# DeltaNet attention with a PReLU feed-forward on one core: weight sums moved from VectorE to GpSimd, late 32x32 products and output copies rearranged

## The chip, the core and the metric

The kernel runs on one core of a Trainium2 chip. A core has five engines, each with its own queue of instructions, worked off in order: TensorE (PE in the profile; its weight loads are shown apart as PEld), VectorE (DVE), ScalarE (ACT), GpSimd (POOL) and SyncE (SP), which here only issues DMAs. Engines wait for each other through semaphores. PE writes its products to PSUM, which has eight banks of 2 KB per partition; DVE and ACT read them from there, and GpSimd works on SBUF alone. The metric is the device time of one execution in microseconds (us).

## What is computed

Everything is float32. First a DeltaNet recurrence over 4 batches, 8 heads, 768 positions, head size 48; then, on the 3072 tokens of width 384 that this gives, a feed-forward of inner width 2048 with a PReLU:

```python
k_n = k / (norm(k) + 1e-6)
for t in range(768):
    y[t] = q[t] @ state                       # per batch and head, state is 48x48
    v_old = k_n[t] @ state
    state = state + beta[t] * outer(k_n[t], v[t] - v_old)
x = y transposed to (4 * 768, 8 * 48)
h = x @ w_in                                  # 384 -> 2048
g = max(h, 0) + alpha * min(h, 0)
out = g @ w_out                               # 2048 -> 384
```

## The kernel before

**Attention in steps.** The recurrence is worked in chunks of 64 positions (`C`). A step n is one chunk of two batches; 12 chunks times 2 pairs of batches give 24 steps, and two steps of one chunk belong to different pairs, so that each pair's state is handed on every other step. Within a chunk the recurrence becomes the inverse of a unit triangular 64x64 matrix for each of 16 batch-heads. Its 32x32 diagonal blocks are inverted on DVE for four steps at once, by column elimination (`eliminate`: 30 pairs of a multiplication, L593, and an addition, L599, both with two operands in SBUF, with transposes at L566 before and after). GpSimd prepares the block for it (L583, L587). The block off the diagonal needs two rounds of 32x32 products on PE (`products`, L733): one for step n+2, whose result ACT copies to `mid`, and one for step n+1, whose result ACT copies to `inv` (`copied`, L745).

**A step's products.** `burst_a(n)` issues to PE the outputs of step n-1 (`outputs`, L840), the product for the next state (`next_state`, L857), and `through_state` (L802). DVE then subtracts from the state (L865, tile `beside`), makes the right side `r` (three instructions at L812) and the masked product `a_t` (L521). `turn_round(n)` issues weights and transposes: DVE's reciprocal (L412) and two small GpSimd instructions (L418, L419) give the weights `wgt` of a later step. `burst_b(n)` issues the query (L784), `solve` (L827) and the 32x32 products; DVE turns the solution into `u` (L831), which the outputs of the next burst need. Up to step 14 `burst_b` also issues the gram product of step n+9 (L501, weighted by DVE at L507 into `same` and `right`). From step 8 on (`NARROW`) the outputs are copied from PSUM by ACT (L846), transposed by DVE (`turn_y`, L881) and put in place by ACT (`rows_y`, L894).

**The feed-forward fills the time between bursts.** The 12 chunks of 256 tokens pass through `ffn_in` (L996; ACT takes the negative part at L1006, DVE adds the two parts at L1008) and `ffn_out`. Chunks 0 and 1 use the plain second product (L1039). From chunk 2 on, `ffn_out_fast` (L1060) takes seven products where eight would be needed, with operands that are sums: of the activations (`operand_sums`, L950, DVE) and of `w_out` (`weight_sums`, L983, DVE, once: eight instructions of 128x768, four for each half b). From chunk 8 on `ffn_in_fast` does the same for the first product; its sums of `w_in` come from `input_sums` (L1162, DVE, once: eight of 128x512, made while chunk 7 passes `ffn_out_fast`). In `ffn_in_fast` ACT copies the shared products (L1264), GpSimd adds them up (L1269), and DVE adds them to the rest (L1274) and applies the slope (L1283).

**What sets the order.** The order on each engine is written out by hand: `weave` interleaves generators by a share of progress, and `stretch(n, ...)` runs n pieces of the feed-forward (`tail`) beside pieces of elimination, of `placing` (L704, L707, L718) and of the list `later` that a burst returns. An engine never overtakes its own queue. So GpSimd begins an instruction as soon as the one before it in its queue and the semaphores allow, whatever DVE is at by then.

**Where the changed pieces stand.** `weight_sums(0, 0, 3)` is woven into step 5, `weight_sums(1, 0, 3)` and `weight_sums(0, 3, 4)` into step 6, `weight_sums(1, 3, 4)` into step 7. Within a half the second sum needs the first, and the last one overwrites a quarter of `w_out`. The product that first reads all eight is in `ffn_out_fast(2)`. `input_sums` has the same form; its two last sums of each half overwrite parts of `w_in` and so must follow `ffn_in(7)`.

**PSUM.** From step 8 on there are two pairs of banks for attention and four single banks for the feed-forward. `ps_big()` hands the pairs out in turn. In `burst_b` the pair `b` takes the solution and the 32x32 products side by side, and the pair `x` takes the gram product and the query; the outputs are later added onto the query in the same columns, and `next_state` writes the first columns of the same pair. Instructions of two engines on one bank are kept apart by semaphores.

Of the kernel before, what the change touches and what calls it, by code (L numbers as in the profile page):

```python
# [28 lines left out]
ALU = mybir.AluOpType  # L29
# [4 lines left out]
HB = 32  # L34
W_IN_P = 512
BUSY = 8
EARLY = 8
FIRST = 6
NARROW = 8
LATE = 16  # L40
# [4 lines left out]
def kernel(  # L45
# [11 lines left out]
    nc = tc.nc  # L57
# [8 lines left out]
    G = H // 2  # L66
# [10 lines left out]
    def ps_big():  # L77

        big.append(big.pop(0))
        return big[-1]  # L80
# [24 lines left out]
    def half(i):  # L105
        return slice(64 * i, 64 * i + 64)

    def dims(i):
        return slice(64 * i, 64 * i + D)
# [5 lines left out]
    N = len(steps)  # L115
# [184 lines left out]
    for t in range(2):  # L300
# [5 lines left out]
        out=ones, in_=ones, compare_op=ALU.is_ge, fill=1.0, base=0,  # L306
# [7 lines left out]
    for t in range(2):  # L314
# [5 lines left out]
        out=first_of, in_=ident.rearrange("p (q u e) -> p u q e", u=2, e=HB // 2)[:, 0],  # L320
# [53 lines left out]
    def by_parity(x):  # L374
        return x.rearrange("p (g a) d -> p a g d", a=2)
# [106 lines left out]
    def quarters():  # L482
        return [(g, a, t) for g in range(G) for a in range(2) for t in range(2)]

    def now(pieces):
        for x in pieces:
            x()

    def region(p, n, **into):

        p = ps_big()[:, :, 0:n] if p is None else p
        assert p.shape[-1] == n
        return p.rearrange("p a (g i) -> p a g i", **into)

    def grams(n, p=None):

        if n >= N:
            return []
        p = region(p, G * C, g=G)
        for g, a, t in quarters():  # L500
            nc.tensor.matmul(  # L501
                p[half(t), a, g], k_t[n][dims(a), g, half(t)], k_t[n][dims(a), g, half(t)]
            )

        def weighted(dst, cols):
            w = stats[n][1][:, 0:2, :, None].to_broadcast([128, 2, G, HB])
            nc.vector.tensor_tensor(  # L507
                out=dst.rearrange("p (a g) i -> p a g i", a=2), in0=p[:, :, :, cols], in1=w,
                op=ALU.mult,
            )  # L510

        return [
            lambda: weighted(gather(n), slice(0, HB)),
            lambda: weighted(right[n % EARLY][:, 1:], slice(HB, C)),
            lambda: keep(n),
        ]
# [21 lines left out]
    def gather(n):  # L538
        m, j = n // NJ, n % NJ
        if j == 0:  # L540
            same[m] = work.tile([128, NJ, H, HB], FP32, name="same", bufs=1)
        return same[m][:, j]
# [180 lines left out]
    def products(n, second, p):  # L723

        to, frm = (0, 1) if second else (1, 0)
        if second:
            x, y = mid[n % 2][:, :, 0:HB], inv[n % NE][:, :, HB:C]
        else:
            x, y = right[n % EARLY][:, 1:], diag[n % NE][:, :, 0:HB]

        def product(i, t):
            rows = quad(2 * t + frm)
            nc.tensor.matmul(p[quad(2 * t + to), i // G, i % G], x[rows, i], y[rows, i])  # L733

        return product
# [13 lines left out]
    def between(*wanted):  # L749

        wanted = [
            (n, second, region(p, G * HB, g=G)) for n, second, p in wanted if n < N
        ]
        todo = [products(*x) for x in wanted]
        for i in range(H):
            for product in todo:
                for t in range(2):
                    product(i, t)
        return [y for x in wanted for y in copied(*x)]
# [8 lines left out]
    nv, rhs_, ys, us, xts, whole = {}, {}, {}, {}, {}, set()  # L768
# [67 lines left out]
    def outputs(n, p=None):  # L836
        c, bp = steps[n]
        p = region(p, G * D, g=G)
        for g, a, t in quarters():
            nc.tensor.matmul(  # L840
                p[half(t), a, g], a_t[n][half(t ^ a), a * G + g], us[n][half(t ^ a), a, g],
                start=(n < NARROW), stop=(n < NARROW or g == G - 1),
            )
        if c == 0 or n >= NARROW:
            ys[n] = work.tile([128, H, D], FP32, name="y")
            return [lambda: nc.scalar.copy(by_parity(ys[n]), p)]  # L846
        return [lambda: nc.vector.tensor_tensor(
            out=by_parity(ys[n]), in0=by_parity(ys[n]), in1=p, op=ALU.add
        )]
# [118 lines left out]
    def weight_sums(b, first, last):  # L968

        n = 3 * (DM // 2)  # L970
        if b == 0:
            flat = space_out.rearrange("p s e -> p (s e)").bitcast(FP32)
        else:
            flat = more.rearrange("p i s e -> p (i s e)")
        t1, t2, t3 = (
            flat.rearrange("p (i x e) -> p x i e", x=3, e=DM // 2)[:, x] for x in range(3)
        )
        own = w_half[:, 4 * b : 4 * b + 4]
        b11, b12, b21, b22 = own[:, :, 0, 0], own[:, :, 0, 1], own[:, :, 1, 0], own[:, :, 1, 1]
        for dst, x, y in (  # L980
            (t1, b12, b11), (t2, b22, t1), (t3, b22, b12), (b12, b21, t2)
        )[first:last]:
            nc.vector.tensor_tensor(out=dst, in0=x, in1=y, op=ALU.subtract)  # L983
            summed.append(b)
            yield

# [162 lines left out]
    def input_sums():  # L1149

        for h in range(2):
            own = [
                w_in[:, t].rearrange("p (i f e) -> p i f e", f=2, e=128)[:, 4 * h : 4 * h + 4]
                for t in range(2)
            ]
            a11, a12, a21, a22 = own[0][:, :, 0], own[1][:, :, 0], own[0][:, :, 1], own[1][:, :, 1]
            s1, s2, s3 = (input_sum(x, h) for x in range(3))
            for dst, x, y, op in (
                (s1, a21, a22, ALU.add), (s2, s1, a11, ALU.subtract),
                (s3, a11, a21, ALU.subtract), (a21, a12, s2, ALU.subtract),  # L1160
            ):
                nc.vector.tensor_tensor(out=dst, in0=x, in1=y, op=op)  # L1162
                yield

    class Due:
# [252 lines left out]
    WY, JOINED = G * D, NJ + 2  # L1418
# [36 lines left out]
    def burst_b(n):  # L1455

        b, x = ps_big(), ps_big()
        gram = grams(n + EARLY + 1, x[:, :, 0 : G * C])
        if n >= NARROW:
            asked_in.append(x)  # L1460
            query(n, x[:, :, G * C : G * C + WY])
        soon = solve(n, b[:, :, 0:WY])
        wanted = [(n + 1, True, b[:, :, WY : WY + G * HB])]
        if n > JOINED:
            wanted.append((n + 2, False, b[:, :, 2 * WY : 2 * WY + G * HB]))
        soon += between(*wanted)
        if n >= LATE:
            now(soon[:1])
            return soon[1:]
        now(soon + gram[:2])  # L1470
        return gram[2:] + [lambda: squares(n + EARLY + 2), lambda: load_early(n + EARLY + 3)]

    def turn_round(n):
# [133 lines left out]
    n = 2 * W_IN_P  # L1607
# [111 lines left out]
    n = 12  # L1719
# [114 lines left out]
    n = WHOLE + PIECES - BEGUN - SOON  # L1834
# [29 lines left out]
    late = ffn_out(1)  # L1864
    few, rest = OUT_PARTS // 4, 11
    n = OUT_PARTS - few - 2 * rest + 1
# [139 lines left out]
```

## Time and profile before

| | |
|---|---|
| median of 3 runs | 645.8 us (644.97 to 646.53) |
| the profiled execution | 645.59 us, span of its instructions 643.9 us |
| granted TensorE clock | 1.00 throughout |
| PE busy | 628.6 us, 98% of the span |
| PEld busy | 552.2 us, 86% |
| DVE busy | 497.9 us, 77% |
| ACT busy | 312.8 us, 49% |
| POOL busy | 92.5 us, 14% |
| PE's share of the chain that ended last | 87% |
| DVE's share of it | 6% |

Times inside the span count from its start. A group of the profile names line, engine, operation, tiles, shapes and count, then the busy time in us and the mean of one in ns, then how long the engine was idle before such instructions and what ended that. A busy PE is not PE at its peak, since ends of matmuls are modelled. The steps that matter below lie so: step 5 from about 159 to 172 us, step 6 to 193, step 7 to 217; step 15 begins at 380, the outputs of step 16 are at 427; the first chunk in `ffn_in_fast` starts at 466.

### The profile page before, as it was taken

The page shows a single profiled execution, that of the slowest core. Times are in us where ns is not written, and L with a number is a line of the kernel's source. Part 1 is how long each engine was busy: PE and PEld are TensorE (multiplying, and loading weights), DVE is VectorE, ACT ScalarE, POOL GpSimd, SP SyncE. Part 2 cuts the span into 40 slices and gives each one's busy share as a digit, 9 for nine tenths or more (in the row PEclk, how much of TensorE's full clock was granted, in tenths as well). Part 3 has the DMA queues.
Part 4 walks back from the last instruction along what each step waited for, and adds up shares of the span by engine and source line. Part 5 has one row for each costly group of instructions (what it writes and reads, how often), then busy time and mean ns, then how long its engine had stood idle before and what let it go on. Part 6 is the DMA issues. An engine that isn't in the chain of part 4 may idle for free.

```text
span 643.9 us, 21686 instructions
## 1 busy us (share of the span) xinstructions
PE 628.6 (98%) x9154; PEld 552.2 (86%) x9154; DVE 497.9 (77%) x1205; ACT 312.8 (49%) x824; POOL 92.5 (14%) x204
## 2 busy tenths in 40 slices
PE   6999999999999999999999999999999999999997
PEld 4687888557778988988988988989989989999997
DVE  4976998977999879858978957978968568576383
ACT  5887565344553243734644635435456366353240
POOL 6001211010000100001000010000044053061360
PEclk9999999999999999999999999999999999999999
DMA  7957735211353242242233121221220300100000
GB/s 119 300 130 169 231 70 153 62 38 31 55 79 54 39 70 44 39 71 45 38 61 55 26 52 26 38 45 19 49 48 8 60 18 6 36 1 2 25 1 25
DMA packets 145969, 39.27 MB, mean 61 GB/s; under 512 B 139040, under 2 KB 142256, under 8 KB 145872
## 3 DMA queue, kind: packets, MB, share of 16 engines
q1 hardware_dynamic: 144000, 37.40, 28.5%
q8 instruction: 72, 1.18, 0.8%
q10 hardware_dynamic: 1872, 0.49, 0.4%
q14 instruction: 25, 0.20, 0.1%
HBM read 33.14 MB, written 4.72 MB: 59 GB/s over the span
## 4 chain that ended last, share of the span: by engine, by line
PE 87%; DVE 6%; DMA 2%; ACT 1%; issue 1%; SPq 1%; POOL 1%; ACTq 0%; DVEq 0%; POOLq 0%
PE p_ffn L996 13%; PE p_ffn L1060 9%; PE p_more L996 8%; PE p_more L1329 8%; PE p_more L1060 8%; PE p_ffn L1039 7%; PE p_more L1245 4%; PE p_ffn L1329 3%; PE p_ffn L1235 3%; PE p_pair L733 2%; PE p_ffn L1240 2%; PE p_pair L802 2%; PE p_pair L840 2%; PE p_pair L1498 2%; PE p_pair L501 2%; PE p_pair L827 2%
## 5 line engine op out<-in xcount | busy, mean ns | idle before, releaser
L996 PE MATMUL p_ffn<-xt,w_in 128*128 128x256 f32 x528 | 124.3, 385 | 2.2 <-DVE act L1008 1.8
L996 PEld LDWEIGHTS p_ffn<-xt,w_in 128*128 128x128 f32 x528 | 97.3, 190 | 17.4 <-issue 1.7
L894 ACT COPY xt<-z 32x96 f32<-32x96 f32 x240 | 64.4, 269 | 43.3 <-DVE z L881 40.2
L745 ACT COPY inv<-p_pair 32x256 f32<-32x256 f32 x40 | 14.5, 362 | 85.3 <-DVE u L831 84.6
L996 PE MATMUL p_more<-xt,w_in 128*128 128x256 f32 x240 | 55.7, 382 | 0.0
L599 DVE TENSOR_TENSOR block<-block,prod 128x30 f32<-128x30 f32 (+9 forms) x150 | 49.8, 332 | 5.2
L1269 POOL TENSOR_TENSOR k_t<-k_t 128x128 f32<-128x128 f32 (+1 forms) x48 | 28.5, 594 | 167.3 <-ACT k_t L1264 164.8
L996 PEld LDWEIGHTS p_more<-xt,w_in 128*128 128x128 f32 x240 | 44.9, 190 | 6.3
L593 DVE TENSOR_TENSOR prod<-block 128x30 f32<-128x30 f32 (+9 forms) x150 | 48.6, 324 | 1.2
L418 POOL TENSOR_TENSOR beta_t<-beta_t,rec 128x8 f32<-128x8 f32 x24 | 6.1, 255 | 271.6 <-DVE rec L412 262.7
L1008 DVE SCALAR_TENSOR_TENSOR act<-act,al_t,p_ffn 128x256 f32<-128x256 f32 x72 | 31.1, 472 | 16.5 <-ACT act L1006 16.5
L1006 ACT ACTIVATE act<-p_ffn 128x512 f32<-128x512 f32 x36 | 21.4, 594 | 24.3 <-PE p_ffn L996 24.0
L1269 POOL TENSOR_TENSOR block<-block 128x128 f32<-128x128 f32 (+1 forms) x48 | 27.6, 575 | 14.1 <-ACT block L1264 11.6
L1235 PE MATMUL p_ffn<-xt,w_in 128*128 128x256 f32 x96 | 29.3, 387 | 0.0
L1060 PE MATMUL p_ffn<-w_out,act 128*128 128x192 f32 x160 | 28.1, 328 | 0.0
L1060 PEld LDWEIGHTS p_ffn<-w_out,act 128*128 128x128 f32 x160 | 26.2, 190 | 0.7 <-DVE act L1008 0.2
L831 DVE TENSOR_TENSOR u<-p_pair,wgt 128x384 f32<-128x384 f32 x24 | 13.2, 554 | 16.9 <-PE p_pair L733 16.0
L812 DVE TENSOR_TENSOR r<-v_raw,p_pair 64x192 f32<-64x192 f32 (+1 forms) x66 | 23.3, 352 | 3.7 <-PE p_pair L802 2.7
L1008 DVE SCALAR_TENSOR_TENSOR act<-act,al_t,p_more 128x256 f32<-128x256 f32 x40 | 17.2, 472 | 11.3 <-ACT act L1006 11.3
L554 ACT COPY same<-right 32x256 f32<-32x256 f32 x29 | 11.7, 403 | 22.6 <-DVE right L507 19.1
L1060 PE MATMUL p_more<-w_out,act 128*128 128x192 f32 x128 | 22.3, 326 | 0.0
L1283 DVE SCALAR_TENSOR_TENSOR act<-k_t,al_t,act 128x256 f32<-128x256 f32 x32 | 19.4, 645 | 3.6 <-ACT k_t L1279 3.5
(255 smaller groups left out, 1474.9 us busy)
## 6 DMA issues: line engine op xcount, KB each, us to landing
w_out<-in_moe_w_in_dram SPq DMA_DIRECT2D x10, 512.0 KB, 4.7
v_raw<-in_v_dram SPq DMA_DIRECT2D x48, 96.0 KB, 2.8
kl<-in_k_dram SPq DMA_DIRECT2D x96, 48.0 KB, 2.4
out_dram<-o_sb SPq DMA_DIRECT2D x90, 48.0 KB, 1.6
space_out<-in_moe_w_out_dram SPq DMA_DIRECT2D x11, 384.0 KB, 3.1
ke_last<-in_k_dram SPq DMA_DIRECT2D x25, 96.0 KB, 3.3
qp<-in_q_dram SPq DMA_DIRECT2D x64, 32.0 KB, 2.3
w_out<-in_moe_w_out_dram SPq DMA_DIRECT2D x5, 384.0 KB, 4.3
```

The lines of the kernel that those rows point to most:

```text
L593: nc.vector.tensor_tensor(out=prod, in0=r[:, 0:j, j : j + 1].to_broadcast([128, j, n]), in1=r[:, j : j + 1, j + 1 : HB].to_broadcast([128, ...
L599: nc.vector.tensor_tensor(out=r[:, 0:j, j + 1 : HB], in0=r[:, 0:j, j + 1 : HB], in1=prod, op=ALU.add)
L812: nc.vector.tensor_tensor(out=r[to, a], in0=v_in[to, a], in1=p[own, a, :, 0:D], op=ALU.subtract)
L894: nc.scalar.copy(to[quad(r), u, bp, t], z[quad(2 * t + u), r])
L996: nc.tensor.matmul(p_h[:, i], w_in[:, t, (f + i) * 128 : (f + i + 1) * 128], xt[:, t], start=(t == 0), stop=(t == KT - 1),)
L1008: nc.vector.scalar_tensor_tensor(out=g[:, i], in0=g[:, i], scalar=al_t[:, f + i : f + i + 1], in1=p_h[:, i], op0=ALU.mult, op1=ALU.add,)
L1039: nc.tensor.matmul(p_o[u], gs[f // 2][:, f % 2, u * 128 : (u + 1) * 128], w_out[:, f], start=(f == 0), stop=(f == FT - 1),)
L1060: nc.tensor.matmul(p, x(i), w(i), start=(i == 0), stop=(i == FP - 1))
L1235: nc.tensor.matmul(p[:, f * 256 : f * 256 + 256], w(2, f), xt[:, 2], start=True, stop=False)
L1245: nc.tensor.matmul(q[:, j], a, b, start=True, stop=True)
L1269: nc.gpsimd.tensor_tensor(out=dst, in0=a, in1=b, op=ALU.add)
L1329: nc.tensor.matmul(p, x(i), w(i), start=(i == 0), stop=(i == FP - 1))
```

## The change

Three edits. The sums of `w_out` and of `w_in` are issued to GpSimd where they were issued to DVE, at the same places of the program. From step 15 on (when no gram product is left to make) the 32x32 products go to the pair `x`, in the columns that the gram product had, and PE gets them ahead of the query and the solution; ACT copies them out as before. From step 16 on DVE, not ACT, copies the outputs from PSUM.

```diff
@@ outputs
         if c == 0 or n >= NARROW:
             ys[n] = work.tile([128, H, D], FP32, name="y")
+            if n >= LATE:
+                return [lambda: nc.vector.tensor_copy(out=by_parity(ys[n]), in_=p)]
             return [lambda: nc.scalar.copy(by_parity(ys[n]), p)]
@@ weight_sums
-            nc.vector.tensor_tensor(out=dst, in0=x, in1=y, op=ALU.subtract)
+            nc.gpsimd.tensor_tensor(out=dst, in0=x, in1=y, op=ALU.subtract)
             summed.append(b)
             yield
@@ input_sums
-                nc.vector.tensor_tensor(out=dst, in0=x, in1=y, op=op)
+                nc.gpsimd.tensor_tensor(out=dst, in0=x, in1=y, op=op)
                 yield
@@ burst_b
         b, x = ps_big(), ps_big()
+        narrow, late = n >= NARROW, n + EARLY + 1 >= N
+        inner = x if late else b
+        at = 0 if late else WY
+        wanted = [(n + 1, True, inner[:, :, at : at + G * HB])]
+        if n > JOINED:
+            wanted.append((n + 2, False, inner[:, :, at + G * HB : at + 2 * G * HB]))
+        copies = between(*wanted) if late else []
         gram = grams(n + EARLY + 1, x[:, :, 0 : G * C])
-        if n >= NARROW:
+        if narrow:
             asked_in.append(x)
             query(n, x[:, :, G * C : G * C + WY])
         soon = solve(n, b[:, :, 0:WY])
-        wanted = [(n + 1, True, b[:, :, WY : WY + G * HB])]
-        if n > JOINED:
-            wanted.append((n + 2, False, b[:, :, 2 * WY : 2 * WY + G * HB]))
-        soon += between(*wanted)
+        if not late:
+            copies = between(*wanted)
         if n >= LATE:
-            now(soon[:1])
-            return soon[1:]
-        now(soon + gram[:2])
+            now(soon)
+            return copies
+        now(soon + copies + gram[:2])
         return gram[2:] + [lambda: squares(n + EARLY + 2), lambda: load_early(n + EARLY + 3)]
```

Here `LATE` is 16, `NARROW` 8, `EARLY` 8, `N` 24, `JOINED` 6, `WY` 192, `G * HB` 128 and `G * C` 256. Seen engine by engine: DVE loses sixteen sums and gains eight copies of 128x384; ACT loses eight copies; POOL gains the sixteen sums; on PE, in steps 15 to 22, the 32 products of 32x32 (16 in step 22) stand ahead of the query's and the solution's 32 instead of behind them. SP's queue is the same.

## Prediction

> **What bounds the kernel now.** I read the engines' shares first, then the busy time by stretches, then the waits.
>
> ```profile
> PE 628.6 (98%) x9154; PEld 552.2 (86%) x9154; DVE 497.9 (77%) x1205; ACT 312.8 (49%) x824; POOL 92.5 (14%) x204
> ```
> ```profile
> 160.00:180.00 20.00, 19.80 (x418) 15.11 (x411) 18.54 (x47) 9.91 (x26) 1.21 (x4) 1.00 0.32 52
> 180.00:200.00 20.00, 19.57 (x323) 16.35 (x322) 19.70 (x49) 8.83 (x23) 0.41 (x2) 1.00 0.51 81
> 200.00:220.00 20.00, 18.64 (x310) 17.13 (x309) 18.16 (x46) 8.01 (x23) 1.83 (x4) 1.00 0.20 33
> 380.00:400.00 20.00, 20.00 (x302) 17.39 (x301) 15.76 (x38) 9.24 (x25) 1.42 (x2) 1.00 0.23 35
> ```
> ```profile
> PE p_ffn L996 <- DVE act L1008: 1.8, 2, 1.4
> ...
> ACT inv L745 <- DVE u L831: 84.6, 17, 9.0
> ```
>
> The stretches give PE, PEld, DVE, ACT, POOL in that order. PE bounds the whole, and its work is not changed; only its idle time can change. From 160 to 207 us DVE is nearly full (19.70 of 20) and PE waits for it: 1.8 us at L996, at 181.75 and 201.96. That is where the sums of `w_out` stand (164 to 203 us). After 340 PE is idle for under 2 us in all. ACT's 84.6 us of waiting for `u` cost PE nothing there: the copies to `inv` and `mid` end 1.9 us or more ahead of the next outputs in every step (471.79 against 473.66 is the closest).
>
> **Sums of `w_out`: what leaves DVE and what comes to GpSimd.**
>
> ```profile
> L983 DVE TENSOR_TENSOR space_out<-w_out 128x768 f32<-128x768 f32 x2 | 1.9, 950 | 0.0
> ```
> ```profile
> L1269 POOL TENSOR_TENSOR block<-block 128x128 f32<-128x128 f32 x32 | 15.4, 481 | 12.9 <-ACT block L1264 11.6
> L1269 POOL TENSOR_TENSOR block<-block 128x256 f32<-128x256 f32 x16 | 12.2, 762 | 1.3
> ```
>
> DVE starts the next instruction 0.87 us after a sum, so eight give it back 7.0 us, 6.1 of it before 201. On GpSimd, 128 more columns cost 0.28 us on 0.20, so 768 take 0.20 + 6 x 0.28 = 1.88 us and 512 take 1.32.
>
> GpSimd does not run free of DVE:
>
> ```profile
> 483.99 0.95 DVE L1283 SCALAR_TENSOR_TENSOR act<-k_t,al_t,act 128x256 f32<-128x256 f32 x1
> ```
> ```profile
> 483.86 0.79 POOL L1269 TENSOR_TENSOR k_t<-k_t 128x256 f32<-128x256 f32 x1
> ```
> ```profile
> 109.90 0.58 DVE L593 TENSOR_TENSOR prod<-block 128x220 f32<-128x220 f32 x1
> ```
> ```profile
> 109.58 0.66 POOL L550 COPY same<-right 32x256 f32<-32x256 f32 x1 [4.29 <-DVE right L507]
> ```
>
> L1283, with two operands in SBUF, takes 0.47 us alone; begun 0.13 after a GpSimd instruction, it ended 0.29 after that one's end (484.65). L593 took 0.58 instead of 0.37 and ended 0.24 after GpSimd's 110.24. `u` (L831), with an operand in PSUM, took its usual 0.56 beside GpSimd at 490.59. So a DVE instruction with two SBUF operands waits out a GpSimd sum, others don't, and GpSimd in turn waits for one such instruction. DVE's elimination here is a row of just such pairs (L593, L599).
>
> The Trainium skill, "SBUF — State Buffer", section "Who interferes with whom", states this as a rule: DVE with two SBUF inputs and a GpSimd instruction that reads SBUF shut each other out for a whole instruction, whichever came first. It speaks against putting the sums beside L593 and L599; by it alone each of the eight could hold DVE for nearly its whole 1.88 us (the far end of rival b, 652.6), and by the rows the same.
>
> The first three sums follow L419 in GpSimd's queue and wait for nothing recent, so they start near 160.95, not at 164:
>
> ```profile
> 160.50 0.36 POOL L419 TENSOR_TENSOR wgt<-beta_t,rec 128x8 f32<-128x8 f32 x1
> ```
> ```profile
> 161.28 0.41 DVE L599 TENSOR_TENSOR block<-block,prod 128x238 f32<-128x238 f32 x1
> 161.60 1.08 DVE L812 TENSOR_TENSOR r<-v_raw,p_pair 128x192 f32<-128x192 f32 x3
> 162.71 0.69 DVE L521 TENSOR_TENSOR a_t<-p_pair,minus 128x512 f32<-128x512 f32 x1
> ...
> 166.60 0.55 DVE L831 TENSOR_TENSOR u<-p_pair,wgt 128x384 f32<-128x384 f32 x1
> ```
> ```profile
> 163.46 0.68 PE L827 MATMUL p_pair<-r,inv 64*64 64x48 f32 x32
> ...
> 167.31 0.68 PE L840 MATMUL p_pair<-u,a_t 64*64 64x48 f32 x32
> ```
>
> PE's L827 starts 0.06 us after `a_t` ends (163.40), L840 0.16 after `u` (167.15): no slack.
>
> Step 5. GpSimd holds from 161.25 to 163.0; L599 at 161.28 ends near 163.2; `a_t` ends 1.5 late. The second sum runs beside `r` and `a_t`, which it doesn't hold up. The third, from 165.2 to 166.9, holds the next L599: 1.6 more. Less one removed sum (0.87), `u` and with it L840 are 1.5 + 1.6 - 0.9 = 2.2 us late. PE loses 2.2; ACT, fed by PE, follows.
>
> Step 6. Two further removed sums bring DVE to +0.7 by 174, but DVE then waits for ACT's norm (+2.2, 0.7 us of idle). The first two sums into `more` follow the `wgt` made from that norm, near 176.6: one holds a L599 for 1.5 us, the other runs beside `r`. The tile that L1008 has to free by 181.31 is ready 2.85 later than in the profile, so PE is 2.85 late. L996 at 184.53 was held 0.2 us by L1008 and no longer is: 2.65.
>
> Step 7. With three more sums gone, DVE is ahead of PE again. The last three (near 187.8 to 193.5) run beside `u`, L507, L1008 and transposes and hold DVE for 0.8. `u` now waits for PE, and L1008 before the stall at 201.96 comes 1.25 late. PE arrives at 200.5 + 2.65 = 203.15 and goes on at 203.2 where it went on at 201.96: the 1.36 us of waiting there is gone, and +1.25 is left. GpSimd's own small work (L418, L419) is in no danger: its `rec` come at 175.6, 186.9 and 209, the sums end at 166.9, 180.5 and 193.5.
>
> **Sums of `w_in`.** Off DVE go 8 x 0.6 us at 451 to 464, where PE waits for nothing: 0. On GpSimd the first three follow L587 (done at 386.03) until about 390, the next four follow PE's last use of half of `w_in` at about 432.5, the last at 445; PE first reads them at 469.5. From 386 to 390 DVE runs instructions with PSUM operands or transposes, which aren't held; at 434 to 438 four of L593 and L599 are held, up to 2.5 us in all, and L1008 behind them has four banks' time (4 x 2.6 us) to spare. Cost 0; if that cover were gone, 2.5.
>
> **Products ahead.** Their 32 matmuls stay, and so does the burst's end, for which `u` waited already. Changes of tile size on PE, from start to start in the trace: before, full to 64 rows 309 ns, to 32 rows 148, to full 121; after, full to 32 rows 309, to 64 rows 121, to full 149: 0. ACT's copies no longer wait for `u`; what follows them (L1264, L894) is set by PE and DVE: 0.
>
> **Copies of the outputs on DVE.** A DVE read of 384 columns in PSUM costs 0.55 us, 0.46 to the next start (L831, L865): 8 x 0.46 = 3.7 us of DVE, with 1.5 us or more to spare up to 466. In the fast stage PE waits for L1264 at 480.08 and 526.73, at the end of a chain that starts with L865, idle until ACT's copy (475.30). DVE can begin its own at 474.75 and L865 at 475.2: about 0.1 less at each. At 497 and 544 the copy adds 0.46 to DVE where 0.4 is spare, 572 has 0.38. Bounds -0.3 to +1.8 (four copies fully exposed); I take -0.2, by the two rows that show a wait.
>
> **Sum.** 645.59 (span 643.9 and 1.7 around it; 0.2 under the median) + 1.25 - 0.2 = 646.65, said as 646.7. About 0.2%, 1.3 us, is what a measurement of this kernel can tell from no change.
>
> **Rivals.**
> (a) GpSimd's reads slip between DVE's instead of shutting them out. Then the 1.8 us at 181.75 and 201.96 go, with 0.3 hidden in matmuls: 643.5; if all 7.0 us of DVE time counted, 638.6. For it: L593 keeps its usual 0.25 us beside an L419 at 301.64; against it: 0.95 for 0.47 at L1283.
> The Trainium skill, "Trainium Kernel Development and Optimization", section "Best Practices", holds the busy time of weight loads a better measure than that of matmuls. By it PE has 3.6 us of room from 160 to 220 (PEld 48.6 of 60, against 52.2 at the share of 380 to 400), and (a) would give 642.0, an estimate.
> (b) The lateness of step 5 and 6 stays. If DVE doesn't get ahead of PE after 187 (a sum holding the last L593 and L599, then `u`, ACT's copies to `inv` and L1006 behind it, which before ended 0.04 us before L1008 needed it), 2.85 + 0.2 remain: 648.6. It decides from a DVE that is over 2.6 us late at 201. At worst each sum holds DVE for 1.75 of its 1.88 us: 8 x (1.75 - 0.87) = 7.0, 652.6. For it: DVE is 98% full there; against it: six sums are gone by then.
> (c) The copies lengthen the fast stage: 1.8 on top of the sum, 648.7. Against it: L865 idles for the copy now.
>
> **Chances.** Forecast 0.47 (its own range 645.4 to 648.0: 0.6 within 0.2%, 0.38 above), (a) 0.22 (0.85 faster, else same), (b) 0.21 (0.95 slower), (c) 0.10 (0.85 slower). Faster: 0.19 + 0.01 = 0.20; same: 0.28 + 0.03 + 0.01 + 0.02 = 0.34; slower: 0.46. The range runs from (a)'s 643.4 to just above (b) and (c), 648.9; about a tenth is left on each side.
>
> **What would show it.** Sums at GpSimd of about 1.9 us, the first near 161; L593 or L599 of 1.5 us or more beside them; PE waiting at L827 and L840 near 164 and 168, longer at 181.75, hardly at 202; no L745 waiting for `u` after 395; PE full from 386 to 450. Wrong if L599 near 161 keeps its 0.41 us, if the sums start later than 164, or if PE's idle time after 466 grows by over 1 us.

## The result and the profile after

The changed kernel took 652.22 us (median of five, 650.55 to 653.50) against 645.46 us for the kernel before on the same chip: a ratio of 1.0101, with a 95% interval of 1.0084 to 1.0117. It is 6.8 us slower; 646.7 had been forecast, and 652.6 as the far end of rival (b), outside the stated range. The profiled execution of the changed kernel took 650.61 us, its span is 648.9 us, 5.0 us more than before. Its granted clock was 1.00 throughout; in the other four it was 0.992 to 0.997 on average, and three of these took 1.6 to 2.9 us longer than the profiled one. So the delay that is followed below, 5 to 6 us, is not quite the whole of the 6.8 us. One execution of w_out_alone (below) took 2972.44 us; it is not in the ratio of that kernel, and the median of its other four is 652.58 us. Line numbers of the changed kernel are 2 higher than before from about L846 on (L996 is now L998, L1008 is L1010, the sums of `w_out` are L985).

The engines' shares, first part of the page of the changed kernel:

```profile
PE 628.0 (97%) x9154; PEld 552.6 (85%) x9154; DVE 503.8 (78%) x1197; ACT 309.1 (48%) x816; POOL 117.9 (18%) x220
```

PE has the same work; only its idle time has grown. DVE gave up 16 sums and took on eight copies of outputs, and yet it is 5.9 us busier than before. The two groups that took the time in, from the costliest groups of the changed kernel (busy us, mean ns, idle before):

```profile
L599 DVE TENSOR_TENSOR block<-block,prod 128x30 f32<-128x30 f32 (+9 forms) x150 | 58.4, 389 | 5.1
...
L593 DVE TENSOR_TENSOR prod<-block 128x30 f32<-128x30 f32 (+9 forms) x150 | 52.4, 350 | 1.3
```

The same two before:

```profile
L599 DVE TENSOR_TENSOR block<-block,prod 128x30 f32<-128x30 f32 (+9 forms) x150 | 49.8, 332 | 5.2
L593 DVE TENSOR_TENSOR prod<-block 128x30 f32<-128x30 f32 (+9 forms) x150 | 48.6, 324 | 1.2
```

The same 300 instructions now last 12.4 us longer. Where PE lost its time, in the stretches (PE, PEld, DVE, ACT, POOL) and in PE's own timeline, which gives the idle time before a row and what ended it:

```profile
160.00:180.00 20.00, 17.75 (x373) 13.09 (x366) 18.79 (x34) 8.26 (x22) 10.38 (x8) 1.00 0.28 48
180.00:200.00 20.00, 15.61 (x248) 12.94 (x250) 17.95 (x41) 8.53 (x22) 5.79 (x5) 1.00 0.45 71
```
```profile
164.33 0.68 PE L827 MATMUL p_pair<-r,inv 64*64 64x48 f32 x32 [1.48 <-DVE a_t L521]
168.82 0.68 PE L840 MATMUL p_pair<-u,a_t 64*64 64x48 f32 x32 [0.57 <-DVE u L831]
...
185.74 3.69 PE L998 MATMUL p_ffn<-xt,w_in 128*128 128x256 f32 x16 [2.81 <-DVE act L1010]
197.22 1.10 PE L998 MATMUL p_ffn<-xt,w_in 128*128 128x256 f32 x4 [1.58 <-DVE act L1010]
207.47 0.89 PE L998 MATMUL p_ffn<-xt,w_in 128*128 128x256 f32 x3 [1.37 <-DVE act L1010]
```

PE's two stalls of this kind before:

```profile
181.75 3.88 PE L996 MATMUL p_ffn<-xt,w_in 128*128 128x256 f32 x16 [0.43 <-DVE act L1008]
201.96 2.83 PE L996 MATMUL p_ffn<-xt,w_in 128*128 128x256 f32 x12 [1.36 <-DVE act L1008]
```

Now there are five. The stall near 202, which was to vanish, is there with its old length, and 1.58 at 197.22 is new. After 220 PE is as full as before.

The reason stands in DVE's and GpSimd's rows side by side (start, duration), step 5, step 6 and step 7 of the changed kernel:

```profile
160.24 2.06 POOL L985 TENSOR_TENSOR space_out<-w_out 128x768 f32<-128x768 f32 x1
160.66 1.90 DVE L599 TENSOR_TENSOR block<-block,prod 128x238 f32<-128x238 f32 x1
162.38 1.85 POOL L985 TENSOR_TENSOR space_out<-w_out,space_out 128x768 f32<-128x768 f32 x1
162.48 1.07 DVE L812 TENSOR_TENSOR r<-v_raw,p_pair 128x192 f32<-128x192 f32 x3
...
164.19 2.08 POOL L985 TENSOR_TENSOR space_out<-w_out 128x768 f32<-128x768 f32 x1
...
164.62 1.90 DVE L599 TENSOR_TENSOR block<-block,prod 128x240 f32<-128x240 f32 x1
...
175.90 1.85 POOL L985 TENSOR_TENSOR more<-w_out 128x768 f32<-128x768 f32 x1
175.91 2.05 DVE L593 TENSOR_TENSOR prod<-block 128x184 f32<-128x184 f32 x1
177.82 1.85 POOL L985 TENSOR_TENSOR more<-w_out,more 128x768 f32<-128x768 f32 x1
177.99 1.89 DVE L599 TENSOR_TENSOR block<-block,prod 128x184 f32<-128x184 f32 x1
...
188.79 1.89 POOL L985 TENSOR_TENSOR more<-w_out 128x768 f32<-128x768 f32 x1
189.01 1.75 DVE L599 TENSOR_TENSOR block<-block,prod 128x58 f32<-128x58 f32 x1
190.64 1.81 POOL L985 TENSOR_TENSOR w_out<-w_out,space_out 128x768 f32<-128x768 f32 x1
...
191.46 1.04 DVE L593 TENSOR_TENSOR prod<-block 128x30 f32<-128x30 f32 x1
192.41 1.81 POOL L985 TENSOR_TENSOR w_out<-w_out,more 128x768 f32<-128x768 f32 x1
192.53 1.75 DVE L599 TENSOR_TENSOR block<-block,prod 128x30 f32<-128x30 f32 x1
```

Seven of the eight sums hold one L593 or L599 until 0.05 to 0.3 us after their own end; the sum at 162.38 alone met `r` (and `a_t` behind it), which have an operand in PSUM and take their usual time. An account of DVE from the L593 at 160.22 to the end of the L1010 that PE waits for at 207.47 (before: from 160.84 to 201.81), worked out from the rows:

| us | before | after | difference |
|---|---|---|---|
| seven sums of `w_out` that stood in the stretch | 6.1 | 0 | -6.1 |
| seven L593 and L599 that are held | 1.8 | 12.0 | +10.2 |
| idle for over 0.1 (waiting for ACT) | 0.8 | 2.3 | +1.4 |
| the rest | 32.2 | 32.8 | +0.6 |
| whole stretch | 41.0 | 47.1 | +6.1 |

DVE was idle for 0.8 us in 41 before and for 2.3 in 47 after: it sets the pace of this stretch in both kernels, and a delay put into it comes out at its end. The reverse is bounded: before, PE waited for DVE for 1.8 us here, and relieving DVE could give back about that much (1.5 us in memsets, below).

### The profile page after: what moved, and what is told of

The parts are those of the page before. It is cut to its first block, busy times and chain, and to the rows that moved or that the text cites. A ratio compares the mean times of both kernels' runs of the same rounds, so it can differ in the third digit from the quotient of the medians.

```text
span 648.9 us, 21709 instructions
## 1 busy us (share of the span) xinstructions
PE 628.0 (97%) x9154; PEld 552.6 (85%) x9154; DVE 503.8 (78%) x1197; ACT 309.1 (48%) x816; POOL 117.9 (18%) x220
## 4 chain that ended last, share of the span: by engine, by line
PE 79%; DVE 11%; ACT 3%; DMA 2%; issue 2%; SPq 1%; POOL 1%; ACTq 0%; DVEq 0%; POOLq 0%
PE p_ffn L998 11%; PE p_ffn L1062 9%; PE p_more L1331 8%; PE p_more L1062 8%; PE p_more L998 7%; PE p_ffn L1041 6%; PE p_more L1247 4%; PE p_ffn L1331 3%; PE p_ffn L1237 3%; PE p_ffn L1242 2%; DVE block L599 2%; PE p_pair L840 2%; PE p_pair L733 2%; PE p_pair L1505 2%; PE p_pair L802 2%
## 5 line engine op out<-in xcount | busy, mean ns | idle before, releaser
L998 PE MATMUL p_ffn<-xt,w_in 128*128 128x256 f32 x528 | 123.9, 384 | 6.0 <-DVE act L1010 5.8
L998 PEld LDWEIGHTS p_ffn<-xt,w_in 128*128 128x128 f32 x528 | 97.5, 190 | 20.8 <-ACT inv L704 3.2
L599 DVE TENSOR_TENSOR block<-block,prod 128x30 f32<-128x30 f32 (+9 forms) x150 | 58.4, 389 | 5.1
L998 PE MATMUL p_more<-xt,w_in 128*128 128x256 f32 x240 | 55.7, 382 | 0.0
L593 DVE TENSOR_TENSOR prod<-block 128x30 f32<-128x30 f32 (+9 forms) x150 | 52.4, 350 | 1.3
L998 PEld LDWEIGHTS p_more<-xt,w_in 128*128 128x128 f32 x240 | 44.9, 190 | 6.3
L1010 DVE SCALAR_TENSOR_TENSOR act<-act,al_t,p_ffn 128x256 f32<-128x256 f32 x72 | 31.0, 471 | 16.2 <-ACT act L1008 16.2
L1008 ACT ACTIVATE act<-p_ffn 128x512 f32<-128x512 f32 x36 | 21.4, 594 | 25.1 <-PE p_ffn L998 24.7
L831 DVE TENSOR_TENSOR u<-p_pair,wgt 128x384 f32<-128x384 f32 x24 | 13.2, 554 | 17.5 <-PE p_pair L827 11.2
L1010 DVE SCALAR_TENSOR_TENSOR act<-act,al_t,p_more 128x256 f32<-128x256 f32 x40 | 17.2, 471 | 9.9 <-ACT act L1008 9.9
L1041 PE MATMUL p_ffn<-w_out,act 128*128 128x384 f32 x64 | 21.8, 491 | 0.4 <-DVE more L1010 0.4
```

What stands on the lines that cost most here:

```text
L593: nc.vector.tensor_tensor(out=prod, in0=r[:, 0:j, j : j + 1].to_broadcast([128, j, n]), in1=r[:, j : j + 1, j + 1 : HB].to_broadcast([128, ...
L599: nc.vector.tensor_tensor(out=r[:, 0:j, j + 1 : HB], in0=r[:, 0:j, j + 1 : HB], in1=prod, op=ALU.add)
L998: nc.tensor.matmul(p_h[:, i], w_in[:, t, (f + i) * 128 : (f + i + 1) * 128], xt[:, t], start=(t == 0), stop=(t == KT - 1),)
L1010: nc.vector.scalar_tensor_tensor(out=g[:, i], in0=g[:, i], scalar=al_t[:, f + i : f + i + 1], in1=p_h[:, i], op0=ALU.mult, op1=ALU.add,)
L1041: nc.tensor.matmul(p_o[u], gs[f // 2][:, f % 2, u * 128 : (u + 1) * 128], w_out[:, f], start=(f == 0), stop=(f == FT - 1),)
```

## The experiments

A run-to-run spread of 2 us and a start that differs by up to 2.3 us from that of the kernel before blur single times. So beside the ratios I use a reading of the traces that leaves the start out: when DVE begins `u` (L831) in each step, against the kernel before, less the same difference in step 4 (150.5 us). In most kernels no changed instruction stands ahead of that; in those with sums moved forward three or six do, and of these only early_on_gpsimd is late in step 4 itself, by 8.3 us. Positive is later.

| kernel | ratio to before (95%) | step 5 | step 6 | step 7 | step 12 | last PE instruction |
|---|---|---|---|---|---|---|
| the change | 1.0101 (1.0084 to 1.0117) | +2.24 | +6.14 | +5.22 | +6.10 | +5.64 |
| w_out_alone | 1.0123 (1.0104 to 1.0141) | +2.24 | +7.02 | +6.12 | +6.80 | +6.78 |
| all_but_w_out | 1.0005 (0.9994 to 1.0015) | 0 | 0 | +0.01 | +0.16 | -0.29 |
| step5_only | 1.0036 (1.0024 to 1.0048) | +2.42 | +1.58 | +1.57 | +1.59 | +1.57 |
| step6_only | 1.0035 (1.0022 to 1.0049) | +0.01 | +1.75 | +2.28 | +2.69 | +2.67 |
| step7_only | 1.0035 (1.0021 to 1.0049) | 0 | +2.71 | +1.86 | +3.03 | +3.03 |
| memsets | 0.9966 (0.9946 to 0.9985) | -0.74 | -2.24 | -2.56 | -1.49 | -1.50 |
| pieces | 1.0002 (0.9990 to 1.0015) | +1.66 | +0.04 | -0.31 | +0.52 | +0.49 |
| early_on_dve | 1.0068 (1.0056 to 1.0080) | +1.99 | +3.63 | +4.16 | +4.56 | +4.56 |
| early_on_gpsimd | 1.0108 (1.0093 to 1.0122) | -0.74 | -2.23 | -1.70 | -1.40 | -1.40 |
| three_early | 0.9980 (0.9967 to 0.9992) | -0.74 | -0.94 | -0.95 | -0.63 | -0.65 |
| five_after | 1.0014 (1.0002 to 1.0025) | -0.75 | +0.84 | -0.03 | +1.15 | +1.13 |
| eight_after | 1.0044 (1.0028 to 1.0059) | -0.75 | +0.84 | +1.26 | +2.34 | +2.32 |
| eight_behind | 0.9988 (0.9971 to 1.0005) | -0.75 | -2.23 | -0.87 | -0.54 | -0.56 |
| five_behind | 0.9978 (0.9962 to 0.9995) | -0.74 | -2.24 | -2.15 | -0.85 | -0.87 |
| five_pieces | 1.0010 (0.9982 to 1.0037) | -0.74 | -2.24 | -1.90 | -0.51 | -0.52 |
| change_behind | 0.9977 (0.9961 to 0.9993) | -0.75 | -2.24 | -2.12 | -0.63 | -1.08 |
| change_early | 0.9988 (0.9974 to 1.0002) | -0.74 | -0.95 | -0.95 | -0.46 | -0.91 |

The row of early_on_gpsimd says only what follows after step 4. Some traces differ from that of the change in one more thing, the granted clock of PE. The row PEclk of a page gives it in tenths of full speed, in 40 slices of the span; here for w_out_alone and for early_on_dve:

```profile
PEclk9999999999889999999999999999999999999999
PEclk9999999999799999999999999999999999999999
```

In w_out_alone the clock is 0.83 from 160 to 170 us and 0.84 from 180 to 190, as 3.4 us at half speed each would give, where the change has 1.00. In the first of them PE's matmuls at L1039 start 0.64 us apart instead of 0.32. The two kernels have the same instructions up to step 14, and yet w_out_alone is 0.88 us later in step 6. step6_only has one such stretch (0.83 from 180 to 190), and in early_on_dve and early_on_gpsimd the clock is 0.51 from 166.5 to 173.4 and from 139 to 146. Each begins within 1.8 us of the end of a wait of PE of 1.5 to 2.8 us, or, in early_on_gpsimd, during one of 6.4. The trace of the change has waits of 1.48 and 2.81 at the same places without it; that the waits bring it on is suggested, not shown. It makes the losses of these four kernels larger than what the sums alone cost. The other traces are free of it from 24 us to the last few instructions.

**Which part of the change.** The kernel before with the sums of `w_out` alone moved, and the change without them:

```diff
# w_out_alone: the kernel before, and only this
-            nc.vector.tensor_tensor(out=dst, in0=x, in1=y, op=ALU.subtract)
+            nc.gpsimd.tensor_tensor(out=dst, in0=x, in1=y, op=ALU.subtract)
# all_but_w_out: the change, and this line of weight_sums put back on nc.vector
```

> Edit: the kernel before, with only the eight sums of w_out on GpSimd. Theory (each sum shuts DVE's L593/L599 out, and nothing else in the change matters): 651.5 to 652.5 us, PE waiting 5 to 6 us for L1008's tile near 182 to 207, as with the whole change. Rival (the sums of w_in, the order of the products or the copies on DVE carry a part): below 649.

> Edit: the changed kernel, with the eight sums of w_out back on DVE. Theory (these three parts cost nothing and bring next to nothing): 644.9 to 645.7 us, PE's waits before 220 as in the kernel before. Rival (the rest costs): 647 or more.

w_out_alone measured 653.14 us (1.0123), all_but_w_out 645.30 (1.0005). The first is 0.6 us above what was expected of it (0.1 by the median of four), the second within. The sums of `w_out` carry the whole loss. The sums of `w_in`, the products ahead and the copies on DVE together change nothing that the times can tell; in the trace they are 0.29 us ahead at the end.

**Which step.** Only some of the eight sums on GpSimd:

```diff
# weight_sums(b, first, last) in the kernel before
-            nc.vector.tensor_tensor(out=dst, in0=x, in1=y, op=ALU.subtract)
+            engine = nc.gpsimd if first == 0 and b == 0 else nc.vector   # step5_only
+            # first == 0 and b == 1: step6_only;  first == 3: step7_only
+            engine.tensor_tensor(out=dst, in0=x, in1=y, op=ALU.subtract)
```

> Edit: the kernel before, with only the first three sums of w_out (step 5) on GpSimd. Forecast's step 5: L840 and PE 2.2 us late. If DVE is late by as much, nothing makes this good before the stall near 182, and the time is 647.0 to 648.0. Rival (what the change costs arises in step 6 and 7, where DVE has no idle time; step 5's delay is taken up by DVE's idle time at 174): under 646.3.

> Edit: the kernel before, with only the three sums into more (issued in step 6) on GpSimd. Theory (the lock goes back and forth, so each sum holds one of L593/L599 for about 1.5 us): 3 x 1.5 less 3 x 0.87 returned, DVE 1.9 us late, 646.7 to 648.2. Rival (the forecast's step 6: only one of the first two holds, and DVE is ahead again by step 7): under 646.3.

> Edit: the kernel before, with only the two last sums (those that overwrite a quarter of w_out, issued in steps 6 and 7) on GpSimd. Theory (each sum holds one of the last small L593/L599 for up to 1.5 us, while u and the last L1008 stand behind): 2 x 1.5 less 2 x 0.87, PE 0.3 to 1.3 us later, 645.5 to 646.8. Rival (the forecast's step 7: held 0.8 in all, and DVE gets ahead of PE, so that the wait of 1.36 near 202 goes): 643.9 to 645.0.

647.29, 647.57 and 648.44 us, ratios of 1.0036, 1.0035 and 1.0035; the first two lie within what was expected. At the last PE instruction they are 1.57, 2.67 and 3.03 us late, 7.3 in all, against 6.78 of all eight together: the delays add up roughly, with a stretch at half clock in step6_only and two in w_out_alone. Of step 5's 2.42 us, 0.84 is made good by step 6, where the stall of 0.43 at 181.75 is gone; what is left then stays to the end. step6_only shows in passing what the forecast had in mind for step 6; DVE and GpSimd in its timeline:

```profile
177.51 2.04 POOL L984 TENSOR_TENSOR more<-w_out 128x768 f32<-128x768 f32 x1
177.87 1.90 DVE L599 TENSOR_TENSOR block<-block,prod 128x184 f32<-128x184 f32 x1
179.63 1.84 POOL L984 TENSOR_TENSOR more<-w_out,more 128x768 f32<-128x768 f32 x1
179.69 1.07 DVE L812 TENSOR_TENSOR r<-v_raw,p_pair 128x192 f32<-128x192 f32 x3
```

Here the first sum met L599, the last of its pair, so that `r` was next on DVE, and the second sum ran beside `r` and `a_t` for nothing. In the whole change the first sum met L593 instead (175.91), and when it let go, that L593's own L599 stood there for the second sum to hold. Which half of a pair a sum meets decides over 1.5 us, and that hangs on tenths of a microsecond. step7_only missed its expectation on the high side (3.03 against 0.3 to 1.3), since a sum on GpSimd met one that was still on DVE, which also has two operands in SBUF; its timeline:

```profile
186.15 1.87 POOL L984 TENSOR_TENSOR w_out<-w_out,space_out 128x768 f32<-128x768 f32 x1
186.28 2.57 DVE L984 TENSOR_TENSOR more<-w_out 128x768 f32<-128x768 f32 x1
...
188.98 1.81 POOL L984 TENSOR_TENSOR w_out<-w_out,more 128x768 f32<-128x768 f32 x1 [0.95 <-PE p_ffn L997]
189.55 1.28 DVE L593 TENSOR_TENSOR prod<-block 128x30 f32<-128x30 f32 x1
```

DVE lost 1.62 and 1.08 us there, and `u`, which in the kernel before began at 188.67, began at 190.99.

**Is it GpSimd's reading, and what does the length of a sum do?**

```diff
# memsets
-            nc.vector.tensor_tensor(out=dst, in0=x, in1=y, op=ALU.subtract)
+            nc.gpsimd.memset(dst, 0.001)
# pieces
-            nc.vector.tensor_tensor(out=dst, in0=x, in1=y, op=ALU.subtract)
+            for i in range(4):
+                nc.gpsimd.tensor_tensor(out=dst[:, i], in0=x[:, i], in1=y[:, i], op=ALU.subtract)
```

> Edit: the kernel before, with the eight sums left out; GpSimd writes a constant into their targets instead, at the places where the change has the sums. Theory (DVE is shut out by GpSimd's reads of SBUF): L599 and L593 keep 0.41 us and less beside a memset, 7.0 us of DVE time are saved, 643.3 to 644.6. Rival (any GpSimd instruction that touches SBUF shuts DVE out, or its writes do): L593/L599 last until the memset ends, and the time follows from the memset's length, above 645 if a memset takes over 1.2 us.

> Edit: as w_out_alone, but each sum on GpSimd in four instructions of 128x192. Theory (the lock is held for one instruction and then passes to the other engine): a piece of some 0.6 us lets one L593/L599 through, so that a whole sum costs DVE 0.8 to 1.1 us where one instruction costs 1.5; less the 0.87 given back DVE is about even, 645.0 to 648.5. Rival (DVE loses in proportion to GpSimd's busy time, which pieces lengthen): 652 or more.

The memsets took 643.49 us, 0.9966. Their timeline, three of them in the first row:

```profile
160.39 2.09 POOL L983 MEMSET space_out<- 128x768 f32 x3
160.41 0.41 DVE L593 TENSOR_TENSOR prod<-block 128x238 f32<-128x238 f32 x1
160.86 0.41 DVE L599 TENSOR_TENSOR block<-block,prod 128x238 f32<-128x238 f32 x1
```

This kernel leaves the sums out. GpSimd writes the same 128x768 elements, and L593 and L599 keep their 0.41 us. So it is GpSimd's reading of SBUF that shuts DVE out. A memset is shorter than a sum (0.70 us from start to start), but long enough to be seen: an L593 begun at 160.41 and held would have lasted 0.7 us or more. The run also gives the price of DVE's sums themselves: without them, and with nothing held, PE is 1.5 us earlier at the end.

The pieces took 645.93 us, 1.0002: the loss is gone although GpSimd does the same work at the same places. From their timeline (four pieces in one row for GpSimd, 0.58 to 0.76 us each):

```profile
163.49 2.56 POOL L984 TENSOR_TENSOR space_out<-w_out,space_out 128x192 f32<-128x192 f32 x4
...
165.64 0.68 DVE L593 TENSOR_TENSOR prod<-block 128x240 f32<-128x240 f32 x1
166.01 2.89 POOL L984 TENSOR_TENSOR space_out<-w_out 128x192 f32<-128x192 f32 x4
166.35 0.68 DVE L599 TENSOR_TENSOR block<-block,prod 128x240 f32<-128x240 f32 x1
```

Each piece here lets one DVE instruction through, which loses 0.27 us (0.68 for 0.41) where a whole sum takes 1.5. L593 and L599 together are 4.4 us longer than before (52.1 and 50.7), not 12.4, while GpSimd is busy for longer than with whole sums (111.5 us, in w_out_alone 107.1). This favours the theory of one instruction at a time over a loss in proportion to GpSimd's busy time.

**Is it the place?** Six sums moved ahead of step 5, on DVE or on GpSimd, then only the three into `space_out`:

```diff
# early_on_dve; early_on_gpsimd has all six at the first place, on nc.gpsimd;
# three_early has the first three only, and leaves the rest where it was
+    for _ in weight_sums(0, 0, 3):
+        pass
     weave(
         (prelude(NJ), 3), (catch_up(EARLY + NJ), 2, 0.1), (part(late, few), few),
...
-        extra = [] if n == NJ else [(weight_sums(0, 0, 3), 3)]
+        extra = []
+        if n == NJ + 1:
+            for _ in weight_sums(1, 0, 3):
+                pass
...
-            extra[1] = [(weight_sums(1, 0, 3), 3)]
```

> Edit: the kernel before, with six of the eight sums of w_out still on DVE, but three of them where DVE idles at 138.7 (3.1 us) and three at the start of step 5, next to an idle time of 2.5 us. Theory (in steps 5 to 7 the time of DVE is what PE waits for, so 5.2 us less work there takes the waits of 0.44 and 1.36 us away): 643.4 to 644.6. Rival (DVE is not the bound there; the waits stay because ACT's and PE's own order sets them): 645.0 or more.

> Edit: the kernel before, with the same six sums on GpSimd, but issued between two eliminations, so that they run from about 125 to 137 us, where PE has its queue full and DVE has 3.9 us of idle time ahead. Theory (sums on GpSimd cost only where DVE has no time to lose): those before 130.7 hold one of L593/L599 each, those beside the transposes from 130.7 on hold nothing, PE waits for nothing before 160, and the 5.2 us taken off DVE bring 643.4 to 644.6. Rival (the sums on GpSimd cost what they cost anywhere): 646.5 or more.

> Edit: the kernel before, all sums on DVE, but the first three (into space_out, which holds nothing else by then) at DVE's idle time near 138.7. Theory (DVE's work from 160 to 202 is what PE waits for): 2.6 us less of it takes the waits at 181.75 and 202 away in part, 643.2 to 644.8. Rival (PE's waits there are not set by the amount of DVE's work): 645.0 or more.

The first two fell far off: 650.35 and 652.82 us. I had overlooked that until about 172 us `more` holds activations of chunk 1; these two kernels overwrite them, so that part of chunk 1's second product is made from sums. That changes numbers and not the instructions, but the places were not what I took them for either. On DVE, the three sums into `more` did not land in the idle time of 2.5 us but behind it, directly ahead of `r`, and PE waited 2.72 us at L827; the half clock right behind that wait (above) took another 3.1 us of PE until L840. On GpSimd, all six met the elimination, which they held so that it never got out of their way:

```profile
125.44 1.95 POOL L984 TENSOR_TENSOR space_out<-w_out 128x768 f32<-128x768 f32 x1
125.76 1.83 DVE L599 TENSOR_TENSOR block<-block,prod 128x184 f32<-128x184 f32 x1
...
134.89 1.93 POOL L984 TENSOR_TENSOR more<-w_out 128x768 f32<-128x768 f32 x1
135.15 1.83 DVE L593 TENSOR_TENSOR prod<-block 128x130 f32<-128x130 f32 x1
```

One DVE instruction to one sum, six times over (four left out above); at 137 the elimination was 9.3 us late, its transposes began at 140.04 instead of 130.74, and PE waited 6.4 us at L1040 for a copy by ACT, until 143.07; the half clock then took 1.4 us more. That the sums would reach the transposes at 130.7 was my error: work that holds DVE pushes the free stretch ahead of itself.

three_early measured 644.77 us, 0.9980: 2.6 us less of DVE's work in the stretch brings 0.65 us by the trace and 1.3 by the ratio, so DVE's work is part of what PE waits for, and only a part of what is taken off it reaches PE. Then GpSimd again, after the last L599, which a one-column copy was to wait for:

```diff
# back(m), run after the elimination's last pair; weight_sums leave steps 5 to 7
         r = block[m]
+        if m == 2:
+            nc.gpsimd.tensor_copy(out=after_block, in_=r[:, 0, 0:1])    # five_after, eight_after
+            # in_=r[:, 0, HB - 1 : HB]: eight_behind, five_behind, five_pieces
+            for x in ((0, 0, 3), (1, 0, 3), (0, 3, 4), (1, 3, 4)):      # five_*: without the first
+                for _ in weight_sums(*x):
+                    pass
```

> Edit: as three_early, and the other five sums on GpSimd, behind a one-column copy of the block that lets them start only after the last L599 of the elimination (near 189), beside DVE's transposes. Theory: at most L950 and L773 are held, once each for up to 1.5 us, against 7.0 us taken off DVE; 642.8 to 644.8. Rival (a sum on GpSimd costs about the same anywhere): 648 or more.

> Edit: the change's part for w_out with one thing different: all eight sums wait for the last L599 of the elimination (near 189) and run to about 204. Theory: three or four of L950 and L773 are held, 1.5 us each at most, behind 6.1 us taken off DVE; 643.0 to 646.0. Rival (a sum on GpSimd costs about the same anywhere, or comes too late for the product that reads it near 204): 648 or more.

> Edit: as eight_after, but the copy that GpSimd's sums wait behind reads the block's last column, which every L599 writes, so that they start after the last L599 (near 188 to 189); in eight_after they had started at 185.4 and held two L599 and one L593. Theory (a sum costs only what it holds): L950 or L773 are held, one to three in all at up to 1.6 us, behind 6.1 us taken off DVE; 643.0 to 645.5, u of step 6 1.5 to 2.7 us earlier than in the kernel before. Rival (running on GpSimd costs PE time wherever it stands): 647 or more, as eight_after.

> Edit: as five_after, with the copy that reads the block's last column: three sums early on DVE, five whole sums on GpSimd after the last L599. Theory: one or two of L950 and L773 held, 642.8 to 644.8. Rival (as above): 646 or more.

> Edit: as five_behind, with each of the five sums in four instructions of 128x192. Theory: what collides with L950 and L773 is held for a piece of 0.6 us at most; as five_behind or up to 1.5 us below it, 642.5 to 644.5. Rival (a whole sum that collides with nothing is no worse than its pieces): the two agree within 0.3 us.

The first two missed: 646.90 and 649.13 us. The column that the copy read is not written by the last L599, so the copy didn't wait for that one, and the sums met the last pairs. The other three have the column that it does write. The same eight sums, in eight_after and in eight_behind, DVE and GpSimd:

```profile
185.42 1.81 POOL L989 TENSOR_TENSOR space_out<-w_out 128x768 f32<-128x768 f32 x1
185.45 1.86 DVE L600 TENSOR_TENSOR block<-block,prod 128x58 f32<-128x58 f32 x1
...
189.20 1.75 DVE L600 TENSOR_TENSOR block<-block,prod 128x30 f32<-128x30 f32 x1
```
```profile
185.42 0.21 DVE L600 TENSOR_TENSOR block<-block,prod 128x30 f32<-128x30 f32 x1
...
186.04 1.81 POOL L989 TENSOR_TENSOR space_out<-w_out 128x768 f32<-128x768 f32 x1 [0.17 <-DMA ke_pair<-in_k_dram]
...
189.67 1.54 DVE L567 STREAM_TRANSPOSE turned<-block 128x256 f32<-128x256 f32 x3
...
191.05 1.03 DVE L956 TENSOR_TENSOR sums<-act 128x512 f32<-128x512 f32 x1
191.49 2.29 POOL L989 TENSOR_TENSOR more<-w_out 128x768 f32<-128x768 f32 x1
```

A start of the sums 2.05 us later (186.04 against 185.42, in traces that stand -0.09 and +1.34 at step 4) makes 1.0044 into 0.9988 (645.08 us). Transposes beside a sum keep their time; L956 (L950 before), with two operands in SBUF, lost 0.35 us here and 0.83 at most (1.51 at 200.81), and made the next sum wait 0.5. So sums on GpSimd cost no more than on DVE where they stand like this, though against leaving them out (memsets, 0.9966) they still cost something. five_behind measured 645.23 (0.9978; 0.4 above the expected range, on a chip where the kernel before took 645.97), five_pieces 645.98 (1.0010; above its expected range too, with an interval of 0.5%, too wide to tell from five_behind; four of its twelve executions had a clock of 0.989 to 0.995 and took 647.8 to 653.0): behind the elimination pieces bring nothing to be seen.

Last, the whole change with its sums of `w_out` moved in these two ways:

> Edit: the whole change, with its sums of w_out as in five_behind (three early on DVE, five on GpSimd after the last L599). Theory (the place of the sums is all that made the change slow): from five_behind's 0.9978 less the 0.3 us that all_but_w_out's trace had at the end, a ratio of 0.996 to 0.999. Rival (the change's other parts cost together with these): above 1.000.

> Edit: the whole change, with its sums of w_out as in three_early (all on DVE, three of them early). Theory: three_early's 0.998 less the same 0.3 us, a ratio of 0.996 to 0.999. Rival: above 1.000.

644.70 us (0.9977, 0.9961 to 0.9993) and 645.01 us (0.9988, up to 1.0002), both within what was expected. The first is faster than both kernels, by some 0.2% than the one before; with five_behind and three_early it forms a group within which these runs don't tell.

## Why the prediction was wrong

The mechanism was forecast; how often it would strike was not. The term that failed is the +1.25 us for the sums of `w_out`: by the traces they cost 5.9 us (5.64 in the change, with 0.29 that its other parts bring). By its steps:

- **GpSimd holds two-operand DVE instructions.** Right, and so is its size: sums of 1.81 to 2.08 us (1.88 said), the first at 160.24 in a trace that starts 0.62 early (160.95 said), a held L599 of 1.90 us. The Trainium skill, "SBUF — State Buffer", section "Who interferes with whom", says further that DVE with two SBUF inputs contends with a GpSimd instruction that reads SBUF and not with one that only writes it; the memsets agree (0.41 us). It says too that DVE with at most one SBUF input, outside the modes that use two ports, doesn't contend; `r` beside a sum agrees (1.07 for three, before 1.08).
- **Step 5: PE 2.2 us late.** Right: `u` 2.24 late in the change, 2.42 in step5_only, by the very instructions named.
- **Step 6: one of two sums holds, 2.65 to 2.85 us late in all.** Wrong. Both held, 1.70 and 1.55. The stall that ended at 181.75 ends at 185.74, 4.6 us later once the early start is added. I had placed the sums by the time of `wgt` and taken one arrangement of pair and sum, which did occur (step6_only), for the one that would.
- **Step 7: 0.8 us held, DVE ahead of PE, the stall of 1.36 gone, +1.25 left.** This is the step that failed most. Three sums held 3.9 us, `u` came behind them, ACT's copies of `inv` and its L1008 wait for `u`, L1010 for that, and PE had a new stall of 1.58 at 197.22. DVE never got ahead, because over the stretch it was given 10.2 us and relieved of 6.1. The stall near 202 kept its length (1.37).
- **Rival (b)** had this mechanism, its place (a sum holding the last L593 and L599, then `u`, ACT, L1008) and its far end of 652.6, which the range left out. Against it I had written that six sums are gone by then; what counts is not that they were gone from DVE but that each came back as a held instruction 1.7 times as dear: 1.5 for 0.87.
- **Rival (a)**, no lock-out: excluded by the held rows. The row given for it, L593 at 301.64, met only the end of an L419 that had itself taken 0.70 us where another took 0.36, behind an L950 begun at 301.04. What it would have been worth is shown by the memsets, 1.5 us at the end of PE's work and 643.49 as measured. The 643.5 worked out from PE's waits was near, and the 642.0 by the rule on weight loads in the Trainium skill, "Trainium Kernel Development and Optimization", section "Best Practices", was not reached: the room of 3.6 us that it gave PE was not there to be had by relieving DVE.
- **Sums of `w_in`: 0.** Right. `u` is +6.10 at step 12 and +6.12 at steps 16, 18 and 19. Three DVE instructions were held in between (0.79, 1.32 and 1.35 us from 440.25 to 443.8, 2.3 us lost of the 2.5 allowed for); `u` of step 17 was 1.9 us later for it (+8.02), and PE never waited.
- **Products ahead: 0.** Right for PE's own order; for ACT it left out a gain. Before, ACT's copies to `inv` waited for `u` (1.20 us, until 491.18), L1279 came behind them at 492.97, DVE's L1283 waited for that, and PE's weight loads of L1329 waited 0.21 us for L1283 at 496.42. In all_but_w_out the copies begin at 490.16, the instruction that was L1279 at 491.95, and PE's wait is gone. The same happens near 543. So L1264 and L894 were not all that follows the copies, and 0.18 us is gained at each of the two places.
- **Copies on DVE: -0.2 (-0.3 to +1.8).** The sign was right, mostly by luck: from step 19 to the end the changed kernel gains 0.48 us, and all_but_w_out 0.47, of which 0.36 is that of the products ahead. Of PE's two waits at L1247, which were to become shorter by 0.1 each, one did (0.50 to 0.42, at 526.47 in all_but_w_out), the other stayed (0.44). Rival (c) is excluded.

## What to carry to other kernels

Before work moves from DVE to GpSimd, look at what DVE will be doing at that moment: an instruction on GpSimd that reads SBUF stops one DVE instruction with two SBUF operands for nearly its whole length, so that a long one beside a row of such instructions costs more than it relieves (here 1.5 us for 0.87). Put it beside transposes and PSUM readers, behind an instruction that it must really wait for, or cut it in pieces. And an engine that is idle for 0.8 us in 41 has no slack by which a delay could vanish: count what it is given against what it is relieved of over the whole stretch, not only the holds one can foresee.

## What the runs showed of the hardware

- With GpSimd's reads and DVE's two-operand instructions both waiting back to back, they alternate one for one: six sums of 1.81 to 1.95 us held six successive instructions for 1.82 to 1.89 us. With pieces of 0.58 us and DVE's 0.41 both engines paid (0.75 and 0.68).
- The holding goes both ways: a sum on GpSimd beside L956 took 2.29 us instead of 1.81.
- Three memsets of 128x768 on GpSimd took 2.09 us together and held nothing.
- Between steps 7 and 8 the change seems to fall back by a further 0.75 us (+5.22 to +5.97), memsets by 0.68 and five_behind by 0.73. This is no time of PE: before, `u` of step 7 begins at 211.41 behind a transpose on DVE and is read by L840 at 217.25 only. PE's difference from before stays constant from 207.6 to 233 us. In step 7 `u` shows where DVE stands, not PE.
- In four kernels the granted clock fell to half for 3.4 or 6.8 us close to the end of a wait of PE of 1.5 to 2.8 us, or during one of 6.4 (0.83 and 0.84 over 10 us in w_out_alone); in the trace of the change it stayed at 1.00 through waits of 1.48 and 2.81.
